# Windowed attention and a gated feed-forward layer: weights converted piece by piece in the order of need, the first steps issued in program order

## The chip, the core and the metric

The kernel runs on one core of one Trainium2 chip. The metric is the device time of the launch in microseconds, as the median of three runs. The profile and its trace come from one profiled execution, whose own time stands in the table below.

## What is computed

```python
def _attn_ref(q, k, v):            # 8 batches, 8 heads, 576 positions, head size 64
    scores = scale * np.matmul(q, k.transpose(0, 1, 3, 2))
    rel = pos[:, None] - pos[None, :]
    mask_plain = (rel >= 0) & (rel < 32)
    mask_dil = (rel >= 0) & (rel < 32 * 4) & (rel % 4 == 0)
    # heads 0 to 3 plain, heads 4 to 7 dilated
    scores = np.where(masks[None], scores, -1e9)
    attn = softmax(scores)
    return np.matmul(attn, v)

def _moe_ref(x, w_in, w_out):      # 4608 tokens, 512 -> 2048 -> 512
    h = x @ w_in
    g = h * np.clip(h + 3.0, 0.0, 6.0) / 6.0
    return g @ w_out
```

The attention's output, with its heads side by side, is the x of the second part. All is float32.

## The kernel before

**The feed-forward part** is cut into 12 chunks c of 384 tokens and 16 blocks f of 128 hidden columns. One step is a pair (c, f). It has a first product gemm1 (lines 407 to 409, twelve matmuls into a PSUM tile ps_h, of which there are two), a stage on ScalarE (ACT) and VectorE (DVE), and a second product gemm2 (lines 428 to 430, nine matmuls into three PSUM tiles ps_o, which add up over all f). Each float32 operand is held as a rounded high part and the remainder, and each product is made of three matmuls: high by high, low by high, high by low. The stage between the products has four instructions: L412 on ACT reads ps_h and writes t, L413 on DVE writes t again, L416 on ACT rounds t into gh, L417 on DVE makes the remainder gl. gemm2 of a step stands two steps behind its gemm1 (LAG).

**The order of the steps.** Chunk 0 leads: the first LEAD steps are (0, 0), (0, 1) and so on, then chunk 0 and chunk 1 take turns, (0, f + LEAD) and (1, f). From step 32 on chunks 2 to 11 follow one another. So a new block f is met first at every second step of this stage, and twice: its first half (from w_in) by gemm1, its second half (from w_out) by gemm2 two steps later.

**The weights.** Each block f has two pieces of 512 KB, its halves. A piece is loaded into a tile st and then converted there into its high and low part in the tile wt of the block: two extractions on ACT (L338, L339) and a shift on DVE (L340), together `cv_fields`; a merge and a custom operation on DVE (L346, L350) and a rounding copy on ACT (L351), together `cv_join`; a subtraction on DVE that makes the low part (L355), `cv_split`. One call of `convert_beat` does one of each for three pieces that follow one another. The pieces are taken in the order of f, both halves of a block together, and gemm1 of a block waits for both (`weights_ready`). All tiles st and wt, and the first nine items' loads, come from one pool of 18 slots.

**The attention** has 48 items (batch, kind of mask, part). An item: scores on TensorE (L163), row maximum, subtraction (L195, L196 on DVE), exponent (L200 on ACT), a transpose of the weights e on TensorE (L242) copied by ACT into a, the product with the values (L173, L181), normalising on DVE (L207, L208, L210), a transpose of the result x, and a split into xh (L299 on ACT) and xl (L302 on POOL), the high and low parts that gemm1 reads. Of the 48 items 12 are done in a start-up of rounds `tau`: round r does the scores of item r, the values of item r - 3, the transposes of e of item r - 1 and of x and the split of item r - 4. Tables by round say where conversion beats (CB) and steps (EARLY) are mixed in. Chunk 0 needs items 0 to 4, chunk 1 items 5 to 9. The other items stand beside later steps, at fixed halves of steps.

**What sets the order on the engines.** The framework's scheduler orders each engine's instructions by a priority number, which `turn_of` sets, and by when it plans their inputs to be ready. All loads are issued by the queue of SyncE (SP), one behind the other.

Names that are used below: round r is `tau`, step n is the n-th pair (c, f), piece k is the k-th half block in the order of conversion, all from 0.

Of the kernel before, what the change touches and what calls it, by code (L numbers as in the profile page):

```python
# [22 lines left out]
TB = 4 * RT  # L23
SPARE = 2
WORK = 12
BEATS = 30
EXTRA = 2
# [12 lines left out]
DEL = 0.2  # L40
G2 = 0.8
EV = -1.9
# [4 lines left out]
def windowed_attention_ffn(ctx: ExitStack, tc: tile.TileContext, qk, vp, w, mask, out):  # L47
# [138 lines left out]
    def softmax(t, ps, masked):  # L186
        e = work_tile("e")
        mx = small.tile([P, SLOTS], F32, name="mx")
        ev = e.rearrange("p (s x) -> p s x", x=2 * QB)
        sv = ps[:, :CH].rearrange("p (s x) -> p s x", x=2 * QB)  # L190
        if not masked:
            _, kind, part = trios[t]
            nc.vector.tensor_tensor(out=e, in0=ps[:, :CH], in1=mask_sb[:, 3 * kind + part], op=ALU.add)
            sv = ev
        nc.vector.tensor_reduce(out=mx, in_=sv, axis=AX.X, op=ALU.max)  # L195
        nc.vector.tensor_tensor(  # L196
            out=ev, in0=sv, in1=mx.rearrange("p (s o) -> p s o", o=1).broadcast_to([P, SLOTS, 2 * QB]),
            op=ALU.subtract,
        )
        nc.scalar.activation(e, e, AF.Exp, scale=SCALE)  # L200
        es[t] = e
        load_qk(t + NLOAD)

    def normalise(t, ps):
        pv = ps[:, : SLOTS * W].rearrange("p (s x) -> p s x", x=W)
# [12 lines left out]
    def blocks():  # L218
        return [(i, u, r) for i in range(SLOTS) for u in range(2) for r in range(2)]

    def st_both(ts, tv):
# [81 lines left out]

    def pace(ins):
# [8 lines left out]

    wt, staged = {}, {}
    WN = w.shape[3]

    def load_w(p):
        st = wpool.tile([P, 4, WN], F32, name="st", tag="w")
# [9 lines left out]
        return words[:, :, 1], words[:, :, 0], st[:, 2], st[:, 3], wt[f][:, 2 * j], wt[f][:, 2 * j + 1]  # L332

    def cv_fields(p):
        if p % 2 == 0:
            wt[p // 2] = wpool.tile([P, 4, WN], F32R, name="wt", tag="w")
        hi_w, lo_w, v, a, _, _ = parts(p)
        pace(nc.scalar.mul(v, hi_w, 2.0**-112))  # L338
        pace(nc.scalar.mul(a.bitcast(U32), lo_w.bitcast(U32), 2.0**-29))  # L339
        nc.vector.tensor_scalar(  # L340
            out=v.bitcast(U32), in0=v.bitcast(U32), scalar1=3, scalar2=None, op0=ALU.logical_shift_left
        )
# [10 lines left out]
    def cv_split(p):  # L353
        _, _, v, _, hi, lo = parts(p)
        nc.vector.tensor_tensor(out=lo, in0=v, in1=hi.bitcast(F32), op=ALU.subtract)  # L355
        del staged[p]


    NP = 2 * NF
    beat = {"loaded": 0, "fields": 0, "join": 0, "split": 0}  # L360

    def load_ahead(n):
        while beat["loaded"] < min(n, NP):
            f = beat["fields"] // 2
            if len(staged) + f + 1 + 1 > NF + SPARE and len(staged) > 0 and beat["loaded"] >= 2:
                break
            load_w(beat["loaded"])
            beat["loaded"] += 1

    def convert_beat():  # L370
        if beat["split"] < beat["join"]:
            cv_split(beat["split"])
            beat["split"] += 1
        if beat["join"] < beat["fields"]:
            cv_join(beat["join"])
            beat["join"] += 1
        p = beat["fields"]
        if p < NP:
            load_ahead(p + 1)
            if p < beat["loaded"]:  # L380
                cv_fields(p)
                beat["fields"] += 1
        load_ahead(p + AHEAD)

    def weights_ready(f):
        while beat["split"] < 2 * (f + 1):
            convert_beat()

    gs, po = {}, {}
# [5 lines left out]
        tc.cur_priority = max(first[0] + int(n * STEP), 0) + 1000  # L395

    def gemm1(n, c, f):
        last["g"] = True
# [5 lines left out]
        for kt in range(NK):  # L404
            a, b = xh[:, kt, r0 : r0 + CH], xl[:, kt, r0 : r0 + CH]
            ks = slice(kt * P, (kt + 1) * P)
            nc.tensor.matmul(ph, lhsT=wt[f][:, 0, ks], rhs=a, start=(kt == 0), stop=False)  # L407
            nc.tensor.matmul(ph, lhsT=wt[f][:, 0, ks], rhs=b, start=False, stop=False)  # L408
            last["pe"] = nc.tensor.matmul(ph, lhsT=wt[f][:, 1, ks], rhs=a, start=False, stop=(kt == NK - 1))  # L409
        turn_of(n + EV)  # L410
        t = work_tile("t")
        nc.scalar.activation(t, ph, AF.Relu, bias=three, scale=1.0)  # L412
# [24 lines left out]
    def first_items(tau):  # L437

        some = lambda t: t if 0 <= t < NFIRST else None
        if some(tau) is not None or some(tau - 3) is not None:  # L440
            st_both(some(tau), some(tau - 3))
        if some(tau - 1) is not None:
            st_turn_e(tau - 1, turn)
        if some(tau - 4) is not None:
            st_turn_x(tau - 4, turn)
            st_split(tau - 4)


    steps = [(0, f) for f in range(LEAD)]
    for f in range(NF):  # L450
        if f + LEAD < NF:
            steps.append((0, f + LEAD))
        steps.append((1, f))
    steps += [(c, f) for c in range(2, NCH) for f in range(NF)]
    beside = {}


# [17 lines left out]
    def step_at(n):  # L475
        c, f = steps[n] if n < len(steps) else (None, None)
        turn_of(n)
        if c is not None:
            gemm1(n, c, f)
        turn_of(n + DEL)  # L480
        for step in beside.get((c, f, 0), []):
            step()
        turn_of(n + 0.4)
        if LEAD <= n < BEATS:
            convert_beat()
        turn_of(n + G2)
        if n >= LAG:
            gemm2(*steps[n - LAG])
# [1 line left out]
        for step in beside.get((c, f, 1), []):  # L490
            step()
        turn_of(n + 0.9)
        if LEAD <= n < BEATS and n % EXTRA == 0:
            convert_beat()

    first[0] = BASE * STEP
    some = P + 2 * CH
# [10 lines left out]
        load_v(t - 2)  # L508
        load_ahead(sum(WITH[: t - 1]))
    n = 0  # L510
    for tau in range(NFIRST + 4):
        turn_of(tau - BASE)
        first_items(tau)
        turn_of(tau - BASE + CD)
        for _ in range(CB.count(tau)):
            convert_beat()
        for _ in range(EARLY.count(tau)):
            step_at(n)
            n += 1
    while n < len(steps) + LAG:  # L520
# [94 lines left out]
```

## Time and profile before

| | us |
|---|---|
| median of 3 runs | 915.86 (915.23 to 916.05) |
| the profiled execution | 915.34 |
| its span, first to last instruction | 913.6 |
| TensorE busy | 891.0 (98%) |
| weight loads of TensorE | 791.6 (87%) |
| VectorE busy | 444.0 (49%) |
| ScalarE busy | 346.5 (38%) |
| POOL busy | 62.5 (7%) |
| mean granted TensorE clock | 0.991 |

Busy times are averages over two stages that differ: a start-up of some 125 us, in which the weights are converted and twelve items done, and a long stage of steps. They are read stage by stage. Matmuls are pipelined, so their busy times overlap; what they cost is read from the starts of neighbours. A wait that the profile ascribes to "issue" is one for which it shows no cause.

### The profile page before, as it was taken

The page shows a single profiled execution, that of the slowest core. Times are in us where ns is not written, and L with a number is a line of the kernel's source. Part 1 is how long each engine was busy: PE and PEld are TensorE (multiplying, and loading weights), DVE is VectorE, ACT ScalarE, POOL GpSimd, SP SyncE. Part 2 cuts the span into 40 slices and gives each one's busy share as a digit, 9 for nine tenths or more (in the row PEclk, how much of TensorE's full clock was granted, in tenths as well). Part 3 has the DMA queues.
Part 4 walks back from the last instruction along what each step waited for, and adds up shares of the span by engine and source line. Part 5 has one row for each costly group of instructions (what it writes and reads, how often), then busy time and mean ns, then how long its engine had stood idle before and what let it go on. Part 6 is the DMA issues. An engine that isn't in the chain of part 4 may idle for free.

```text
span 913.6 us, 20574 instructions
## 1 busy us (share of the span) xinstructions
PE 891.0 (98%) x8732; PEld 791.6 (87%) x8732; DVE 444.0 (49%) x934; ACT 346.5 (38%) x661; POOL 62.5 (7%) x77
## 2 busy tenths in 40 slices
PE   6897999999999999999999999999999999999998
PEld 4576999989889899899888989988888998899996
DVE  3899983244545454444454445445444544422221
ACT  2778862333333333233333223233333332332322
POOL 0212100000010110000000000000100010000000
PEclk9799999999999999999999999999999999999999
DMA  9927430022313222222122123113211310100000
GB/s 354 386 83 260 140 93 0 1 95 89 86 54 119 72 70 81 66 67 84 47 85 85 48 64 104 51 46 99 71 49 52 116 32 11 45 5 1 36 1 34
DMA packets 37820, 74.87 MB, mean 82 GB/s; under 512 B 7264, under 2 KB 16608, under 8 KB 37728
## 3 DMA queue, kind: packets, MB, share of 16 engines
q1 hardware_dynamic: 32544, 64.12, 21.8%
q10 hardware_dynamic: 5184, 9.44, 2.7%
q8 instruction: 68, 1.11, 0.5%
q14 instruction: 24, 0.20, 0.1%
HBM read 57.02 MB, written 9.44 MB: 73 GB/s over the span
## 4 chain that ended last, share of the span: by engine, by line
PE 92%; DMA 4%; DVE 2%; ACT 1%; issue 0%; SPq 0%; POOL 0%
PE ps_o L428 15%; PE ps_h L407 15%; PE ps_h L409 14%; PE ps_h L408 14%; PE ps_o L429 14%; PE ps_o L430 14%; PE ps_a L181 3%; PE ps_a L163 2%; DMA first<-in_v 2%; DMA st<-in_w 1%; DMA v<-in_v 1%; DVE st L350 1%; DVE st L346 1%; DVE wt L355 0%; PE ps_a L242 0%
## 5 line engine op out<-in xcount | busy, mean ns | idle before, releaser
L413 DVE SCALAR_TENSOR_TENSOR t<-t,ps_h 128x384 f32<-128x384 f32 x192 | 106.3, 554 | 326.0 <-ACT t L412 325.8
L407 PE MATMUL ps_h<-xh,wt 128*128 128x384 f32 x768 | 261.5, 341 | 2.9 <-DVE t L413 2.8
L408 PE MATMUL ps_h<-xl,wt 128*128 128x384 f32 x768 | 259.9, 338 | 0.5 <-POOL xl L302 0.5
L409 PE MATMUL ps_h<-xh,wt 128*128 128x384 f32 x768 | 259.9, 338 | 0.0
L428 PE MATMUL ps_o<-wt,gh 128*128 128x512 f32 x576 | 228.7, 397 | 2.0 <-ACT gh L416 2.0
L429 PE MATMUL ps_o<-wt,gh 128*128 128x512 f32 x576 | 224.9, 390 | 0.0
L430 PE MATMUL ps_o<-wt,gl 128*128 128x512 f32 x576 | 221.3, 391 | 0.6 <-DVE gl L417 0.6
L412 ACT ACTIVATE t<-ps_h,three 128x384 f32<-128x384 f32 x192 | 111.1, 579 | 273.3 <-PE ps_h L409 273.0
L417 DVE TENSOR_TENSOR gl<-t,gh 128x384 fp32r<-128x384 f32 x192 | 107.0, 557 | 101.4 <-ACT gh L416 100.1
L407 PEld LDWEIGHTS ps_h<-xh,wt 128*128 128x128 f32 x768 | 144.9, 189 | 11.8 <-DVE t L413 3.3
L408 PEld LDWEIGHTS ps_h<-xl,wt 128*128 128x128 f32 x768 | 144.9, 189 | 8.7 <-POOL xl L302 0.6
L409 PEld LDWEIGHTS ps_h<-xh,wt 128*128 128x128 f32 x768 | 145.0, 189 | 0.8 <-issue 0.3
L416 ACT CAST gh<-t 128x384 fp32r<-128x384 f32 x192 | 98.5, 513 | 111.3 <-DVE t L413 109.1
L430 PEld LDWEIGHTS ps_o<-wt,gl 128*128 128x128 f32 x576 | 108.2, 188 | 24.2 <-DVE gl L417 1.0
L428 PEld LDWEIGHTS ps_o<-wt,gh 128*128 128x128 f32 x576 | 108.3, 188 | 20.1 <-ACT gh L416 2.3
L429 PEld LDWEIGHTS ps_o<-wt,gh 128*128 128x128 f32 x576 | 108.4, 188 | 15.7
L302 POOL TENSOR_TENSOR xl<-xf,xh 128x384 fp32r<-128x384 f32 (+3 forms) x72 | 62.2, 877 | 740.6 <-ACT xh L299 671.8
L200 ACT ACTIVATE e<-e 128x384 f32<-128x384 f32 x48 | 25.2, 526 | 112.4 <-DVE e L196 112.3
L163 PE MATMUL ps_a<-kq 64*32 64x64 f32 x1872 | 47.1, 225 | 0.0
L299 ACT CAST xh<-xf 128x384 fp32r<-128x384 f32 (+3 forms) x72 | 33.7, 536 | 34.7 <-DMA xf<-xf_t 34.6
L181 PEld LDWEIGHTS ps_a<-v,a 64*32 64x32 f32 x1728 | 35.8, 105 | 9.2 <-issue 8.6
L181 PE MATMUL ps_a<-v,a 64*32 64x65 f32 x1728 | 41.6, 225 | 0.0
(45 smaller groups left out, 494.6 us busy)
## 6 DMA issues: line engine op xcount, KB each, us to landing
st<-in_w SPq DMA_DIRECT2D x32, 512.0 KB, 5.7
kq<-in_qk SPq DMA_DIRECT2D x39, 416.0 KB, 4.5
v<-in_v SPq DMA_DIRECT2D x39, 390.0 KB, 3.5
out<-o ACTq DMA_DIRECT2D x36, 256.0 KB, 2.9
first<-in_qk SPq DMA_DIRECT2D x9, 416.0 KB, 8.0
first<-in_v SPq DMA_DIRECT2D x9, 390.0 KB, 8.5
a<-a_t SPq DMA_DIRECT2D x144, 24.0 KB, 1.8
xf<-xf_t SPq DMA_DIRECT2D x144, 24.0 KB, 1.8
```

Of the source, the lines that this page charges most:

```text
L163: last["pe"] = nc.tensor.matmul(ps[at : at + QB, 2 * QB * i : 2 * QB * (i + 1)], lhsT=x[rows, KW + QB * n : KW + QB * (n + 1)], rhs=x[rows ...
L181: last["pe"] = nc.tensor.matmul(ps[at : at + QB, i * W : (i + 1) * W], lhsT=ats[t][rows, QB * n : QB * (n + 1)], rhs=vs[t][rows, n, :], st ...
L407: nc.tensor.matmul(ph, lhsT=wt[f][:, 0, ks], rhs=a, start=(kt == 0), stop=False)
L408: nc.tensor.matmul(ph, lhsT=wt[f][:, 0, ks], rhs=b, start=False, stop=False)
L409: last["pe"] = nc.tensor.matmul(ph, lhsT=wt[f][:, 1, ks], rhs=a, start=False, stop=(kt == NK - 1))
L412: nc.scalar.activation(t, ph, AF.Relu, bias=three, scale=1.0)
L413: nc.vector.scalar_tensor_tensor(out=t, in0=t, scalar=6.0, in1=ph, op0=ALU.min, op1=ALU.mult)
L416: nc.scalar.copy(gh, t)
L417: nc.vector.tensor_tensor(out=gl, in0=t, in1=gh.bitcast(F32), op=ALU.subtract)
L428: nc.tensor.matmul(po[c][tt], lhsT=gh[:, ts], rhs=wt[f][:, 2], start=(f == 0), stop=False)
L429: nc.tensor.matmul(po[c][tt], lhsT=gh[:, ts], rhs=wt[f][:, 3], start=False, stop=False)
L430: last["pe"] = nc.tensor.matmul(po[c][tt], lhsT=gl[:, ts], rhs=wt[f][:, 2], start=False, stop=(f == NF - 1))
```

## The change

- The pieces are taken in the order in which gemm1 and gemm2 first need them (`pieces`): f0 first half, f1 first, f2 first, f0 second, f3 first, f1 second, f2 second, f4 first, f3 second, f5 first and so on. gemm1 waits for the first half of its block alone, gemm2 for the second.
- LEAD is 3 in place of 4. CB has ten beats in rounds 5 to 13 in place of fourteen in rounds 6 to 12, EARLY six steps in place of nine. From step 6 on each step has one beat, between its gemm1 and the reading of its product; the beats that were set by BEATS and EXTRA go.
- Within a beat the order is now: extractions of piece b, merge of piece b - 1, split of piece b - 2, shift of piece b. Where no slot is free for the load of piece b, the split comes first and the load behind it.
- The first loads carry one weight piece per item (WITH), eight in all, where there were up to two and twelve.
- TensorE's instructions stand in program order in the whole kernel, those of DVE and ACT in the rounds and the steps before step 28 (ORDERED).
- In a round the scores' maximum and subtraction come before the normalising, the transposes are placed ahead of the exponent, and the split of x behind the normalising.

```diff
-LEAD = 4
+LEAD = 3
-WITH = (0, 0, 0, 0, 2, 0, 2, 0, 2, 2, 2, 2)
-CB = (6, 6, 7, 7, 8, 8, 9, 9, 10, 10, 11, 11, 12, 12)
+WITH = (0, 0, 0, 0, 1, 1, 1, 1, 1, 1, 1, 1)
+CB = (5, 6, 7, 8, 9, 10, 11, 11, 12, 13)
-EARLY = (8, 9, 10, 11, 12, 13, 14, 15, 15)
+EARLY = (8, 9, 11, 13, 14, 15)
+ORDERED = 28
...
+        if ts is not None:
+            softmax(ts, ps, masked)
+        if between is not None:
+            between()
+        if ts is not None:
+            exponent(ts)
         if tv is not None:
             normalise(tv, pv)
-        if ts is not None:
-            softmax(ts, ps, masked)
...
+    pieces = sorted(range(2 * NF), key=lambda p: (when[p // 2] + LAG * (p % 2), p % 2))
...
     def load_ahead(n):
         while beat["loaded"] < min(n, NP):
-            f = beat["fields"] // 2
-            if len(staged) + f + 1 + 1 > NF + SPARE and len(staged) > 0 and beat["loaded"] >= 2:
+            free = NF + SPARE - len(staged) - len(wt)
+            if len(staged) > 0 and beat["loaded"] >= 2 and free < 1 + (len(wt) < NF):
                 break
-            load_w(beat["loaded"])
+            load_w(pieces[beat["loaded"]])
             beat["loaded"] += 1
...
+        load_ahead(b + 1)
+        full = beat["loaded"] < min(b + 1, NP)
+        if full:
+            cv_split(pieces[b - 2])
+            load_ahead(b + 1)
+        if b < NP:
+            assert b < beat["loaded"]
+            cv_fields(pieces[b])
+        if 0 <= b - 1 < NP:
+            cv_join(pieces[b - 1])
+        if 0 <= b - 2 < NP and not full:
+            cv_split(pieces[b - 2])
+        if b < NP:
+            cv_shift(pieces[b])
+        load_ahead(b + 1 + AHEAD)
...
-        weights_ready(f)
+        weights_ready(2 * f)
...
     def gemm2(c, f):
+        weights_ready(2 * f + 1)
...
         if c is not None:
-            gemm1(n, c, f)
+            ph = gemm1(n, c, f)
+        turn_of(n + 0.4)
+        if n >= len(EARLY):
+            convert_beat()
+        if c is not None:
+            act(n, c, f, ph)
...
-        if LEAD <= n < BEATS and n % EXTRA == 0:
-            convert_beat()
...
+    with tc.manual_schedule(engines={mybir.EngineType.Activation, mybir.EngineType.DVE}):
+        for tau in range(NFIRST + 4):
...
+        while n < ORDERED:
             step_at(n)
             n += 1
...
-        windowed_attention_ffn(tc, *args, o)
+        with tc.manual_schedule(engines={mybir.EngineType.PE}):
+            windowed_attention_ffn(tc, *args, o)
```

The line numbers of the new kernel are shifted: L360, L366, L370 and L375 are the old L340, L346, L350 and L355; L442 and L446 the old L413 and L417.

The order on DVE at the second half of block f3, which gemm2 of step 3 reads. Before, with wt_853 the tile of f3 and t_989 and gl_993 the outputs of step 2:

```order
L417 TENSOR_TENSOR gl_881<-t_877,gh_880 128x384
L346 SCALAR_TENSOR_TENSOR st_151<-st_151 128x512
L355 TENSOR_TENSOR wt_853<-st_145,wt_853 128x512
L350 ISA st_149<-st_149 128x1024
L210 TENSOR_TENSOR x_938<-ps_a_885,z_935 128x384
L196 TENSOR_TENSOR e_940<-ps_a_884,mx_941 128x384
L350 ISA st_151<-st_151 128x1024
L413 SCALAR_TENSOR_TENSOR t_989<-t_989,ps_h_976 128x384
```

And now, with wt_831 the tile of f3, and t_1266 and t_1303 the outputs of steps 4 and 5:

```order
L442 SCALAR_TENSOR_TENSOR t_1266<-t_1266,ps_h_1253 128x384
L446 TENSOR_TENSOR gl_1270<-t_1266,gh_1269 128x384
L442 SCALAR_TENSOR_TENSOR t_1303<-t_1303,ps_h_1290 128x384
L446 TENSOR_TENSOR gl_1307<-t_1303,gh_1306 128x384
L366 SCALAR_TENSOR_TENSOR st_1031<-st_1031 128x512
L370 ISA st_1031<-st_1031 128x1024
L375 TENSOR_TENSOR wt_831<-st_943,wt_831 128x512
```

The subtraction that makes the low part of f3's second half stood ahead of step 2's output, and stands behind step 5's now.

The order on DVE at the second half of block f14. Before, with wt_1711 the tile of f14, and t_1739 and t_1785 the outputs of steps 14 and 15 (f14 is first met by step 24):

```order
L413 SCALAR_TENSOR_TENSOR t_1739<-t_1739,ps_h_1726 128x384
L355 TENSOR_TENSOR wt_1711<-st_1669,wt_1711 128x512
L350 ISA st_1715<-st_1715 128x1024
L417 TENSOR_TENSOR gl_1743<-t_1739,gh_1742 128x384
L413 SCALAR_TENSOR_TENSOR t_1785<-t_1785,ps_h_1772 128x384
L340 TENSOR_SCALAR st_1766<-st_1766 128x512
L346 SCALAR_TENSOR_TENSOR st_1766<-st_1766 128x512
L355 TENSOR_TENSOR wt_1711<-st_1715,wt_1711 128x512
```

And now, with wt_2034 the tile of f15, wt_1956 that of f14, t_2079 and t_2117 the outputs of steps 25 and 26, and st_2032, st_2071 and st_2109 the last three pieces, 29 to 31 (gemm2 of step 25 reads f14 behind gemm1 of step 27):

```order
L442 SCALAR_TENSOR_TENSOR t_2079<-t_2079,ps_h_2057 128x384
L446 TENSOR_TENSOR gl_2083<-t_2079,gh_2082 128x384
L375 TENSOR_TENSOR wt_2034<-st_2032,wt_2034 128x512
L366 SCALAR_TENSOR_TENSOR st_2071<-st_2071 128x512
L370 ISA st_2071<-st_2071 128x1024
L360 TENSOR_SCALAR st_2109<-st_2109 128x512
L442 SCALAR_TENSOR_TENSOR t_2117<-t_2117,ps_h_2095 128x384
L446 TENSOR_TENSOR gl_2121<-t_2117,gh_2120 128x384
L366 SCALAR_TENSOR_TENSOR st_2109<-st_2109 128x512
L370 ISA st_2109<-st_2109 128x1024
L375 TENSOR_TENSOR wt_1956<-st_2071,wt_1956 128x512
```

The last load, of piece 31 into st_2109, takes the slot of st_2032 and waits for its subtraction. On ACT the two extractions of st_2109 stand ahead of the reading of step 26's product, so on DVE everything from the third last of these groups on follows them.

More of the change, by code (lines that the diff above doesn't have):

```diff
@@ L25 @@
 WORK = 12
-BEATS = 30
-EXTRA = 2
 WARM = 8
@@ L302, in st_split @@
             eng.tensor_tensor(out=view(xl), in0=src, in1=view(xh).bitcast(F32), op=ALU.subtract)
+    steps = [(0, f) for f in range(LEAD)]
+    for f in range(NF):
+        if f + LEAD < NF:
+            steps.append((0, f + LEAD))
+        steps.append((1, f))
+    steps += [(c, f) for c in range(2, NCH) for f in range(NF)]
+    when = {f: steps.index((0, f)) for f in range(NF)}
     def pace(ins):
@@ L334, in cv_fields, with cv_shift @@
     def cv_fields(p):
[L335 removed]
+        if p // 2 not in wt:
             wt[p // 2] = wpool.tile([P, 4, WN], F32R, name="wt", tag="w")
         hi_w, lo_w, v, a, _, _ = parts(p)
[L338 to L339 removed]
+        nc.scalar.mul(v, hi_w, 2.0**-112)
+        nc.scalar.mul(a.bitcast(U32), lo_w.bitcast(U32), 2.0**-29)
+    def cv_shift(p):
+        v = parts(p)[2]
         nc.vector.tensor_scalar(
@@ L439, in first_items, with between @@
         some = lambda t: t if 0 <= t < NFIRST else None
[L440 to L443, printed above, removed]
+        def between():
+            if some(tau - 1) is not None:
+                st_turn_e(tau - 1, turn)
+            if some(tau - 4) is not None:
+                st_turn_x(tau - 4, turn)
+        st_both(some(tau), some(tau - 3), between)
         if some(tau - 4) is not None:
-            st_turn_x(tau - 4, turn)
             st_split(tau - 4)
[L449 to L454, printed above, removed]
     beside = {}
```

52 lines of the change are left out of this document (22 added, 30 removed).

## The prediction

> **What bounds the kernel now.** I read the busy time by stage first, then what TensorE (PE) waited for, then the starts of one marker instruction. In the first view the columns are busy time (and instructions) of PE, weight loads, VectorE (DVE), ScalarE (ACT) and POOL, then the granted clock and the DMA share.
>
> ```profile
> 30.00:40.00 10.00, 8.03 (x110) 4.93 (x117) 9.42 (x20) 8.09 (x17) 3.54 (x4) 0.65 1.02 404
> 110.00:120.00 10.00, 10.00 (x52) 9.12 (x51) 10.00 (x20) 7.39 (x14) 0.00 (x0) 1.00 0.34 107
> 200.00:300.00 100.00, 100.00 (x1044) 89.78 (x1044) 51.05 (x114) 34.88 (x68) 8.19 (x10) 1.00 0.29 89
> ```
> ```profile
> PE ps_a L173 <- issue: 9.3, 4, 3.8
> PE ps_h L407 <- DVE t L413: 2.8, 1, 2.8
> ```
>
> From 110 us on PE never pauses; every wait of the whole program lies in the start-up. So the change can win only there, and lose there or wherever it makes PE wait anew. L412 reads each step's finished first product, so its starts tell when product n ended (I call that E(n)). These are steps 6, 16 and 20:
>
> ```profile
> 90.77 0.58 ACT L412 ACTIVATE t<-ps_h,three 128x384 f32<-128x384 f32 x1
> ...
> 131.46 0.58 ACT L412 ACTIVATE t<-ps_h,three 128x384 f32<-128x384 f32 x1 [1.51 <-PE ps_h L409]
> ...
> 147.97 0.58 ACT L412 ACTIVATE t<-ps_h,three 128x384 f32<-128x384 f32 x1 [2.41 <-PE ps_h L409]
> ```
>
> Steps 16 to 20 are (147.97 - 131.46)/4 = 4.13 us apart, PE's own pace. Carried back, a program already at that pace would have E(6) = 147.97 - 14 x 4.13 = 90.15. Both programs do the same PE work behind step 6 (the 12 items are done by then, one transpose apart), so the result is **E(6) of the change against 90.15, plus any new wait behind it**.
>
> **The start-up, step by step.** DVE's groups in the first 125 us (busy, mean ns):
>
> ```profile
> L350 DVE CUSTOM_DVE_ANT_0 st<-st 128x1024 uint16<-128x1024 uint16 x29 | 22.1, 764 | 0.0
> L346 DVE SCALAR_TENSOR_TENSOR st<-st 128x512 uint32<-128x512 uint32 x30 | 22.0, 732 | 0.2
> L355 DVE TENSOR_TENSOR wt<-st,wt 128x512 fp32r<-128x512 f32 x28 | 20.7, 742 | 1.4 <-ACT wt L351 1.4
> L340 DVE TENSOR_SCALAR st<-st 128x512 uint32<-128x512 uint32 x30 | 13.3, 445 | 2.2 <-ACT st L338 2.1
> L413 DVE SCALAR_TENSOR_TENSOR t<-t,ps_h 128x384 f32<-128x384 f32 x14 | 7.6, 546 | 1.7 <-ACT t L412 1.7
> L417 DVE TENSOR_TENSOR gl<-t,gh 128x384 fp32r<-128x384 f32 x14 | 7.6, 545 | 0.0
> L210 DVE TENSOR_TENSOR x<-ps_a,z 128x384 f32<-128x384 f32 x12 | 6.6, 550 | 0.2
> L195 DVE TENSOR_REDUCE mx<-ps_a 128x6 f32<-128x384 f32 x12 | 6.6, 549 | 4.5 <-PE ps_a L163 4.5
> L196 DVE TENSOR_TENSOR e<-ps_a,mx 128x384 f32<-128x384 f32 x12 | 6.6, 549 | 0.1
> L208 DVE RECIPROCAL z<-z 128x6 f32<-128x6 f32 x12 | 2.2, 180 | 0.0
> L207 DVE TENSOR_SCALAR z<-ps_a 128x6 f32<-128x6 f32 x12 | 1.9, 157 | 8.5 <-PE ps_a L173 6.1 <-PE ps_a L163 2.5
> ```
>
> A piece costs DVE 0.764 + 0.732 + 0.742 + 0.445 = 2.68, an item 3 x 0.55 + 0.34 = 1.99 (1.10 of it scores, 0.89 normalising), a step 1.09. What the change removes: in the first 87.3 us, up to the read of product 5, the old order has split 15 pieces (one L355 each, the row below); the new one has split 8 by then, so 7 x 2.68 = 18.8 us of DVE work leave the start-up.
>
> ```profile
> L355 DVE TENSOR_TENSOR wt<-st,wt x15: 644/682/1222, 31.6 to 83.9; 128x512 fp32r<-128x512 f32 x15
> ```
>
> What it adds is waiting, because DVE and ACT now run in program order and L417 stands right behind L413 with ACT's cast between them:
>
> ```profile
> 131.94 0.61 ACT L351 CAST wt<-st 128x512 fp32r<-128x512 f32 x1
> 132.66 0.51 ACT L416 CAST gh<-t 128x384 fp32r<-128x384 f32 x1
> 134.04 0.66 ACT L338 ACTIVATE st<-st 128x512 f32<-128x512 f32 x1 [0.86 <-DMA st<-in_w]
> ```
> ```profile
> 132.08 0.56 DVE L413 SCALAR_TENSOR_TENSOR t<-t,ps_h 128x384 f32<-128x384 f32 x1 [0.74 <-ACT t L412]
> 132.59 0.69 DVE L355 TENSOR_TENSOR wt<-st,wt 128x512 fp32r<-128x512 f32 x1
> 133.21 0.56 DVE L417 TENSOR_TENSOR gl<-t,gh 128x384 fp32r<-128x384 f32 x1
> ```
>
> Step 16 reads: product read 131.46, gl finished 133.77, so **E to gl is 2.31 us** and L413 to the end of L417 is 1.69. The old order puts another piece's split into the hole; the new one leaves it empty.
>
> Where round 7 begins is not changed by this edit, since PE stands still there for a reason that no semaphore shows:
>
> ```profile
> 31.98 0.21 PE L173 MATMUL ps_a<-first,a 64*32 64x65 f32 x1 [3.42 <-issue]
> ```
> ```profile
> 16.00:25.30 9.30, 5.34 (x126) 4.12 (x127) 3.24 (x10) 3.04 (x7) 1.00 (x1) 0.82 1.03 408
> 25.30:29.00 3.70, 2.69 (x127) 2.17 (x127) 2.08 (x5) 3.22 (x6) 1.00 (x1) 1.00 1.02 403
> ```
>
> Between two such waits lie 126 to 127 matmuls with as many weight loads, while the DMA engines are full (1.02): I read it as the instruction stream waiting behind the data. The new order has the same instructions up to there. [...]
>
> So round 7's scores end at about 32.8 and DVE goes on, each round with an item and a piece 1.99 + 2.68 = 4.67, each step 1.69 more: round 7 ends 37.5. Round 8 has step 0, which needs the last of item 4: scores done 38.6; the exponent and two casts to xh, taken as 0.5 each like the cast above, to 40.1; xl on POOL, which starts inside the casts, to 41.6;
>
> ```profile
> 38.35 1.85 POOL L302 TENSOR_TENSOR xl<-xf,xh 128x192 fp32r<-128x192 f32 x2 [4.07 <-ACT xh L299]
> ```
>
> the last five matmuls at the low clock of that stage (0.65) to 43.2; t and gl to 45.5, while DVE had nothing else to do from 42.1. Round 9 ends 51.9, round 10 56.5, round 11 (two pieces, one step) 65.6, round 12 (no scores) 69.2, round 13 74.4, round 14's normalising 75.3; then the last transpose and half a step of PE: **E(5) = 78.0**. Bounds: gap-free DVE work from 32.8 is 5 x 1.99 + 3 x 0.89 + 8 x 2.68 + 5 x 1.09 = 39.5, hence 72.3; further waits of ACT in order could add 4, hence 82.
>
> Then the first new wait. gemm2 of step 3 stands behind product 5 on PE, and needs the split of piece 8, which DVE has behind t and gl of step 5: 2.31 + 0.73 + 0.76 + 0.74 less three overlaps of 0.1, less the first matmul (0.23), which needs the other half: **4.0 us of idle PE**. What such a gap does to the clock is seen once:
>
> ```profile
> 90.00 0.44 PE L407 MATMUL ps_h<-xh,wt 128*128 128x384 f32 x1 [2.82 <-DVE t L413]
> ```
> ```profile
> 91.00:92.00 1.00, 1.00 (x5) 1.00 (x4) 1.00 (x4) 1.00 (x3) 0.00 (x0) 0.53 1.03 422
> 92.00:93.00 1.00, 1.00 (x5) 1.00 (x4) 1.00 (x3) 0.27 (x1) 0.66 (x1) 0.50 1.13 369
> 93.00:94.00 1.00, 1.00 (x6) 0.91 (x5) 1.00 (x3) 0.49 (x2) 0.88 (x1) 0.50 0.79 315
> 94.00:95.00 1.00, 1.00 (x4) 0.80 (x4) 1.00 (x3) 1.00 (x3) 0.00 (x0) 0.76 0.28 115
> ```
> ```profile
> 75.69 0.50 PE L428 MATMUL ps_o<-wt,gh 128*128 128x512 f32 x1 [1.98 <-ACT gh L416]
> ```
>
> 2.82 us of idling were followed by a clock of 0.50 to 0.76, which loses 0.47 + 0.50 + 0.50 + 0.24 = 1.7 us; 1.98 us were not. I take 1.7 for 4 us (bounds 0 and 1.7). So E(6) = 78.0 + 4.13 + 4.0 + 1.7 = 87.8: **2.3 us won**.
>
> **Behind the start-up.** Steps 6 to 26 convert one piece each with ACT in order: L413's wait, gl, join, custom operation, ACT's cast of that piece, and only then the next step's read. That ring is 2.31 + 0.73 + 0.76 + 0.61 = 4.41 without overlap and about 4.1 with 0.1 at each of three seams; against PE's 4.13 it costs between 0 and 0.28 x 20 = 5.6. I take a ring of 4.20, near the overlapped end as neighbouring rows overlap: **1.3 us lost**. The cover is thin: any slip of DVE in a step is PE's.
>
> The last piece is late. Its load takes the place of piece 29 and waits for that split, which stands behind gl of step 25; the landing time of such late loads is
>
> ```profile
> DMA to landing us min/median/max: 3.3/3.7/5.1
> ```
>
> From E(25): gl 2.31, split 0.74, landing 3.7, then ACT in order: two extractions and a cast, 0.57 apart each, 8.5; product 26 is read only then, gl of step 26 at 10.8, join 12.1, split of piece 30 at 12.7. PE wants that split for gemm2 of step 25 at 2 x 4.13 + 0.23 = 8.5: **4.2 us of idling and 1.7 of clock lost** (with 3.3 for the landing 3.8). Before, f14's second half was split some ten steps ahead, so nothing waited. Steps 24 and 25 meet the same wait for pieces 29 and 30, but read their product 0.1 us late only.
>
> Setting PE to program order in the long stage costs nothing by the 200 to 300 us row: items stand at the same halves, gl is done 2.31 after its product and read 8.3 after it.
>
> Sum: -2.3 + 1.3 + 4.2 + 1.7 = +4.9 on the profiled execution's 915.34 (span 913.6 and 1.7 around it): 920.2. The median of the runs, 915.86, is 0.5 higher: **920.5**.
>
> **The rivals.**
> A, faster or equal: the 18.8 us come through. The mechanism is DVE alone in rounds 7 to 14: if ACT and POOL are always ahead and its operations start 0.51 to 0.60 apart as L413 and L355 above do, E(5) comes between 65 and 72.3, and the result is 907 to 915, around 911. It decides from E(5) below 73. For it: DVE is at 9.42 of 10 us in the 30 to 40 us row, so work taken away is time. Against it: the empty holes of each step, and step 0 that cannot be earlier than item 4's xl.
> B, the last load is not late, for the queue finds its slot sooner: 914.6. The order of the split before that load speaks against it.
> C, the fetch wait goes, as the change loads 8 pieces where 12 were loaded at once: round 7 could begin near 30, where DVE's sums for round 6 end, 2.8 earlier, so 917.7. Against: at 32 us neither order has emptied its queue. [...]
> D, PE in program order waits in the long stage, 0.3 us in each of the 36 later items: 931. Nothing in the rows is for it.
> E, gaps of 4 us do not lower the clock, as the 1.98 us one did not: 917.1.
>
> **How the numbers follow.** Forecast 0.50 (its own range 917 to 925), A 0.26, B 0.04, C 0.07, D 0.06, E 0.07. A change below 0.2% (1.8 us) can't be told from none here. Faster: A without its upper end, 0.23; same: that end, B and most of E, 0.13; slower: the rest, 0.64. The range 911 to 926 takes in A's middle, both bounds of E(5) and of the ring, and leaves out D.
>
> **What would show it.** E(5) near 78 and E(6) near 88 by the product reads; two PE waits of about 4 us, the first on the second half of f3, the second near 177 us on f14's; a clock of 0.5 behind each; steps 7 to 23 at 4.13 to 4.25. Wrong it is if E(6) lies before 83, if there is no wait near 177 us, or if PE waits anywhere behind it.

## The result, and the profile after

The change makes the kernel slower. Its median is 930.26 us (930.06 to 932.13, 4 runs) against 915.95 (915.23 to 917.91, 4 runs), a ratio of 1.0157 with a 95% interval of 1.0137 to 1.0178. The direction was forecast, the size was not: 4.9 us more were predicted and 14.3 came, beyond the range (911 to 926). In the profiled executions the span goes from 913.6 to 928.5, by 14.9 us. They are split up below.

What TensorE waited for from 60 us on (us in total, times, longest):

```profile
PE ps_o L459 <- DVE wt L375: 7.8, 2, 4.2
PE ps_a L172 <- ACT a L250: 4.6, 1, 4.6
PE ps_o L458 <- ACT wt L371: 2.1, 1, 2.1
PE ps_a L180 <- DMA a<-a_t: 0.3, 1, 0.3
```

The reads of products 5, 6, 25, 27 and 28 on ACT (start, duration, and in brackets the idle time ahead):

```profile
83.93 0.58 ACT L441 ACTIVATE t<-ps_h,three 128x384 f32<-128x384 f32 x1 [1.08 <-PE ps_h L435]
94.77 0.58 ACT L441 ACTIVATE t<-ps_h,three 128x384 f32<-128x384 f32 x1 [3.99 <-PE ps_h L435]
...
177.42 0.57 ACT L441 ACTIVATE t<-ps_h,three 128x384 f32<-128x384 f32 x1
...
190.02 0.58 ACT L441 ACTIVATE t<-ps_h,three 128x384 f32<-128x384 f32 x1
196.87 0.58 ACT L441 ACTIVATE t<-ps_h,three 128x384 f32<-128x384 f32 x1 [5.01 <-PE ps_h L435]
```

The two places of the waits on PE, on f3's second half and on f14's:

```profile
88.29 0.79 PE L459 MATMUL ps_o<-wt,gh 128*128 128x512 f32 x1 [4.16 <-DVE wt L375]
...
185.98 0.50 PE L458 MATMUL ps_o<-wt,gh 128*128 128x512 f32 x1 [2.13 <-ACT wt L371]
190.12 0.80 PE L459 MATMUL ps_o<-wt,gh 128*128 128x512 f32 x1 [3.64 <-DVE wt L375]
```

The table of stages again, with PE's busy time first and the granted clock behind POOL's:

```profile
180.00:190.00 10.00, 4.35 (x21) 3.43 (x19) 4.99 (x9) 3.22 (x6) 0.00 (x0) 0.94 0.15 52
190.00:200.00 10.00, 9.88 (x37) 8.74 (x38) 2.89 (x6) 2.21 (x5) 0.00 (x0) 0.72 0.00 0
200.00:300.00 100.00, 99.67 (x1086) 89.17 (x1085) 48.01 (x109) 35.65 (x69) 7.18 (x9) 1.00 0.30 91
```

So both waits are at the steps where they were forecast, the second one 7 us and more later in time than the forecast's 177 us, and the long stage is full again. The accounts by the prediction's terms:

| term | predicted | measured | from |
|---|---|---|---|
| product 6 against 90.15 | -2.3 | +4.6 | 94.77 |
| of it: product 5 | at 78.0 | at 83.93 | its read |
| of it: idle, then low clock | 4.0 + 1.7 | 4.16 + 2.55 | 94.77 - 83.93 - 4.13 = 6.71 |
| steps 7 to 27 | +1.3 | +2.4 | 85.0 from product to product start, less 20 x 4.13 |
| wait at step 27: idle, low clock | 4.2 + 1.7 | 6.2 + 2.65 | 12.99 from product 27's end to 28's, less 4.13 |
| long stage and end | 0 | -0.95 | reads 15.9 apart at step 28, spans 14.9 |
| sum | +4.9 | +14.9 | |

The first idle time is that of the view, whose matmul ends are modelled; the second is counted from the starts (the view has 2.13 + 3.64 = 5.77 for it). By the starts the first is 4.33, and 2.4 are left for the low clock behind it.

### The profile page after: what moved, and what is told of

It is laid out like the page before. It is cut to its first block, busy times and chain, and to the rows that moved or that the text cites. A ratio compares the mean times of both kernels' runs of the same rounds, so it can differ in the third digit from the quotient of the medians.

```text
span 928.5 us, 20496 instructions
## 1 busy us (share of the span) xinstructions
PE 892.3 (96%) x8732; PEld 795.1 (86%) x8732; DVE 444.2 (48%) x934; ACT 349.1 (38%) x661; POOL 61.5 (7%) x77
## 4 chain that ended last, share of the span: by engine, by line
PE 87%; DVE 5%; ACT 3%; issue 2%; DMA 1%; SPq 1%; POOL 0%; ACTq 0%; DVEq 0%
PE ps_o L458 14%; PE ps_h L433 14%; PE ps_o L459 13%; PE ps_h L434 13%; PE ps_h L435 13%; PE ps_o L460 13%; PE ps_a L180 3%; PE ps_a L162 2%; DVE st L370 1%; DVE st L366 1%; PE ps_a L247 1%; PE ps_a L172 1%; ACT t L441 1%; DVE t L442 1%; ACT gh L445 1%
## 5 line engine op out<-in xcount | busy, mean ns | idle before, releaser
L442 DVE SCALAR_TENSOR_TENSOR t<-t,ps_h 128x384 f32<-128x384 f32 x192 | 106.4, 554 | 330.1 <-ACT t L441 330.1
L459 PE MATMUL ps_o<-wt,gh 128*128 128x512 f32 x576 | 227.2, 394 | 7.8 <-DVE wt L375 7.8
L458 PE MATMUL ps_o<-wt,gh 128*128 128x512 f32 x576 | 228.9, 397 | 2.1 <-ACT wt L371 2.1
L460 PE MATMUL ps_o<-wt,gl 128*128 128x512 f32 x576 | 226.0, 392 | 0.0
L441 ACT ACTIVATE t<-ps_h,three 128x384 f32<-128x384 f32 x192 | 111.4, 580 | 267.6 <-PE ps_h L435 266.4
L446 DVE TENSOR_TENSOR gl<-t,gh 128x384 fp32r<-128x384 f32 x192 | 107.2, 558 | 115.2 <-ACT gh L445 114.0
L459 PEld LDWEIGHTS ps_o<-wt,gh 128*128 128x128 f32 x576 | 109.0, 189 | 27.4 <-DVE wt L375 11.6
L460 PEld LDWEIGHTS ps_o<-wt,gl 128*128 128x128 f32 x576 | 109.0, 189 | 22.9
L458 PEld LDWEIGHTS ps_o<-wt,gh 128*128 128x128 f32 x576 | 108.7, 189 | 20.8 <-ACT wt L371 2.5
L162 PE MATMUL ps_a<-kq 64*32 64x64 f32 x1872 | 45.9, 225 | 0.0
```

Of the source, the lines that this page charges most:

```text
L162: last["pe"] = nc.tensor.matmul(ps[at : at + QB, 2 * QB * i : 2 * QB * (i + 1)], lhsT=x[rows, KW + QB * n : KW + QB * (n + 1)], rhs=x[rows ...
L442: nc.vector.scalar_tensor_tensor(out=t, in0=t, scalar=6.0, in1=ph, op0=ALU.min, op1=ALU.mult)
L446: nc.vector.tensor_tensor(out=gl, in0=t, in1=gh.bitcast(F32), op=ALU.subtract)
L458: nc.tensor.matmul(po[c][tt], lhsT=gh[:, ts], rhs=wt[f][:, 2], start=(f == 0), stop=False)
L459: nc.tensor.matmul(po[c][tt], lhsT=gh[:, ts], rhs=wt[f][:, 3], start=False, stop=False)
L460: last["pe"] = nc.tensor.matmul(po[c][tt], lhsT=gl[:, ts], rhs=wt[f][:, 2], start=False, stop=(f == NF - 1))
```

## Experiments

Theory L of the runs is the prediction's own idea pushed on: TensorE waits because single splits stand too late on VectorE, and each wait is by itself. Its rivals vary: a shared limit (S), the ring of VectorE and ScalarE (R), the landing of the last load (Q). "Start" means the read of product 1: orders that are the same up to there had it between 51.25 and 53.89 in ten profiles, so a single span says nothing below some 1.3 us either way, and the place is read instead. Runs 1 to 9, 12 and 13 are one execution each; runs 10, 11, 14 and 15 are medians of 6 to 12.

**1. One beat ahead of step 5's outputs.**

```diff
-        if n >= len(EARLY):
+        if n >= len(EARLY) - 1:
```

> One conversion beat moves from behind step 5's outputs to ahead of them; nothing else moves. Theory L (lateness: TensorE waits because the split of a piece stands one beat too late, and each such wait stands by itself): the wait on f3's second half goes, with 4.2 us of idling and 2.5 us of low clock behind it; the read of product 6 moves from 94.77 to about 88.1, the wait near 184 to 190 us on f14 stays as it is, span 928.5 to about 921.8. Rival S (the start-up is VectorE's sum of work, so a beat that is done earlier delays step 5's outputs and the same wait comes back at step 6 or 7): product 6 read later than 92, span 926 to 929.

Measured: span 924.1. The same place on PE:

```profile
85.63 0.50 PE L459 MATMUL ps_o<-wt,gh 128*128 128x512 f32 x1 [0.52 <-DVE wt L375]
```

From product 1 to product 6 it takes 37.14 us in place of 42.49: 5.3 of the 6.7 come back, and the wait on f14 stays. Product 6 is read at 89.86, against 88.1 by L and over 92 by S: L holds and S falls. L's span was 2.3 too low: product 5 comes 1.0 later counted from product 1 (32.65 against 31.65), the start is 0.4 later, and the stage behind step 28 takes 0.8 longer.

**2. One beat in each of rounds 5 to 14.**

```diff
-CB = (5, 6, 7, 8, 9, 10, 11, 11, 12, 13)
+CB = (5, 6, 7, 8, 9, 10, 11, 12, 13, 14)
```

> The second of the two beats of round 11 moves behind step 2's outputs (one beat in each of rounds 5 to 14). The number of beats ahead of step 5 stays. Theory P (in program order ScalarE reads product 2 only behind two beats; TensorE idles 4.6 us for the copy of item 11's weights that stands behind that read, and runs without a pause from there to product 5): product 2 is read at about 64 instead of 66.70, product 5 at about 81.2 instead of 83.93, span about 925.8. Rival S (the sum of VectorE's work up to product 5 sets it): product 5 stays within 0.5 us of 83.93, span 928 to 929.

Measured: span 929.2, with the start 1.6 us later (53.89 against 52.28). From product 1 to product 5: 29.70 in place of 31.65, and of the idle 4.6 us 1.6 are left:

```profile
67.71 0.94 PE L172 MATMUL ps_a<-v,a 64*32 64x65 f32 x48 [1.56 <-ACT a L250]
```

P is right by 2.0 of its 2.7 us, counted from product 1. By its own signs the rival S was met (product 5 at 83.59, and a span over 928): with the start 1.6 us later, neither sign could tell the two apart.

**3. One more beat ahead.** The edit of run 1, and `15` at the end of CB.

> The edit of the first of these runs, and one more beat ahead of step 5, so that every later beat comes one step earlier. Theory L: f3's wait goes (6.7 us), the 0.25 us that gemm2 of every odd step from 7 to 25 waits for a split of its own step goes (2.4 us), and at step 27 the split of piece 30 is due 0.4 us late in place of 6.2 us of idling and 2.65 of low clock (8.4 us won): span about 911.0. Rival R (the ring of ScalarE and VectorE in program order costs its 0.1 to 0.3 us in each step whatever the lead): steps 7 to 27 stay at 4.25, span about 913.4. Rival Q (ScalarE standing behind the landing of the last load holds back the outputs of whatever step it falls into): TensorE waits 4 us or more near step 26 to 28 again, span 916 to 920.

Measured: span 921.1, ten above L and 1.1 above Q's range. The 0.25 us at the odd steps are gone, against R. The beat more ahead is paid for in the start-up: from product 1 to product 6 it takes 39.88 us, 2.7 more than in run 1. And PE now waits for product 25's output (VectorE's L442), which stands behind ScalarE's wait for the last load, as Q had it:

```profile
178.01 0.66 ACT L355 ACTIVATE st<-st 128x512 f32<-128x512 f32 x1 [5.11 <-DMA st<-in_w]
...
179.64 0.58 ACT L441 ACTIVATE t<-ps_h,three 128x384 f32<-128x384 f32 x1
```
```profile
180.86 0.44 PE L433 MATMUL ps_h<-xh,wt 128*128 128x384 f32 x1 [4.06 <-DVE t L442]
```

**4. TensorE in program order to step 27 only.** `EngineType.PE` moves from the block around the whole kernel into the block that ends at step 28.

> TensorE keeps program order through the rounds and steps 0 to 27 and is ordered by the framework from step 28 on. Theory T (the order of TensorE in the long stage costs nothing, and saves 0.85 us at the very end, since the last step's three output tiles end one after the other rather than together): steps 28 to 191 as far apart as in both kernels, span about 929.3. Rival D of the prediction (0.3 us of waiting in each of the 36 later items): span about 918.

Measured: span 923.2, less than the first theory and more than D. Product 27 is read at 189.85 (190.02 in the change), and product 46 is read 9.6 us behind the kernel before, against 15.8 in the change: 6 us won between. At the end of the span it is still 9.6, where the change has won some 0.9 back. I had overlooked that the free order has an effect at step 28 itself. PE takes product 28 in the middle of the wait on f14:

```profile
185.81 0.50 PE L458 MATMUL ps_o<-wt,gh 128*128 128x512 f32 x1 [2.08 <-ACT wt L371]
186.88 0.44 PE L433 MATMUL ps_h<-xh,wt 128*128 128x384 f32 x1 [0.57 <-DVE t L442]
```

D falls by the change's own trace: at step 46 and at step 190 alike its product is read 15.8 us behind the kernel before, so the items between cost nothing.

**5. The next split between the two VectorE instructions of an output, from step 6 on.**

```diff
+        if n >= HOLE and beat["at"] - 2 < NP: cv_split(pieces[beat["at"] - 2])
```

(in `act`, behind L442, with HOLE = 6; the beat leaves that split out.)

> From step 6 on the split of the piece that is next in line stands on VectorE between the two instructions of a step's output (L442, L446), in the 0.65 us that VectorE waits there for ScalarE's rounding; before it stood behind the next piece's merge and custom operation. Nothing else moves, on no engine. Theory V (VectorE's own program order is what is late: its cycle of 1.13 + 0.48 + 0.72 + 0.61 + 0.60 + 0.42 + 0.23 = 4.19 us, and 4.8 where the split stands ahead of a load, is longer than TensorE's 4.13, so that the splits come late at every odd step and the last load by over 2 us): the cycle falls to some 3.6, the odd steps' 0.25 goes (2.4 us), the wait of 6.2 us and the low clock of 2.65 behind it near f14 go; up to product 6 nothing changes; span about 917.2, give or take 1 for the start. Rival R (ScalarE's chain sets the cycle): steps at 4.25 as before and a wait of 3 us or more on f14, span 922 or more.

Measured: span 921.6, start 0.6 later. The odd steps' loss is gone. In the waits view it had never stood, since the modelled end of a pipelined matmul covers a gap of 0.1 us; the starts of neighbours show it. The change first (L458 to L459 0.36 us, L459 to L460 0.34), then this run (0.23 and 0.23):

```profile
98.69 0.40 PE L458 MATMUL ps_o<-wt,gh 128*128 128x512 f32 x1
99.05 0.50 PE L459 MATMUL ps_o<-wt,gh 128*128 128x512 f32 x1
99.39 0.39 PE L460 MATMUL ps_o<-wt,gl 128*128 128x512 f32 x1
```
```profile
100.20 0.39 PE L458 MATMUL ps_o<-wt,gh 128*128 128x512 f32 x1
100.43 0.39 PE L459 MATMUL ps_o<-wt,gh 128*128 128x512 f32 x1
100.66 0.39 PE L460 MATMUL ps_o<-wt,gl 128*128 128x512 f32 x1
```

V is right on that. On f14 2.2 us are left, and the products are still read 4.21 us apart, each a little later behind its end (0.1 us at product 7, 1.6 at product 25): R is right on the cycle, which runs through ScalarE, and on the span.

**6. VectorE and ScalarE in the framework's order from step 6 on.** `ORDERED = 6`.

> VectorE and ScalarE keep program order to step 5 only; from step 6 the framework orders them, TensorE as in the change. Theory V (what costs behind step 6 is the fixed order on VectorE, with its empty hole): the waits at odd steps and on f14 go as in the run before this one, span 916 to 919. Rival L2 (the conversion is one beat short whatever the order within a step): the wait on f14 stays at 4 us or more, span 924 or more.

Measured: span 918.2; products 8 to 28 read 4.13 apart, and no wait for a split behind f3's. V holds, L2 falls.

**7. TensorE in the framework's order throughout.**

> The framework orders TensorE in the whole kernel; ScalarE and VectorE as in the change. Theory H (each late split costs as much as it does since TensorE, in program order, cannot take the next product while it waits): from 5 us at f14 alone, which the run with program order to step 28 has shown, to 11 of the 15.6 us of both waits come back, span 918 to 924. Rival T2 (the splits are late by themselves, and another order only moves the wait): f3's wait stays above 3 us and the span above 926, or the framework's order of the rounds costs more than it gives.

Measured: span 920.1, within H's range. From product 1 to product 6: 38.17 in place of 42.49; single waits are smaller (3.2 us the longest behind 60 us, on f14; at most 1.6 elsewhere). H holds, T2 falls.

**8. POOL's part of the start-up on VectorE.** `ONV = tuple(range(12))`.

> The low part of x of the first twelve items is made on VectorE instead of POOL. Theory C (VectorE's two-input operations take 0.5 to 0.9 us longer while POOL works on its subtraction; 6.2 us in all between 30 and 77 us in the changed kernel, where the prediction had 1.8): with POOL empty all custom operations of the rounds take 0.69 and all splits and merges 0.68, and the 12 items add some 7 us of VectorE's own work, so that product 5 is read within 2 us of 83.93. Rival M (the long ones come from the full DMA or from waits inside the operation): durations of 1.2 to 1.4 stay, and product 5 is read 4 us or more later.

Measured: span 929.8, product 5 at 84.06. The custom operation between 27 and 78 us (shortest/median/longest ns), in the change and in this run:

```profile
L370 DVE CUSTOM_DVE_ANT_0 st<-st x9: 692/1209/1379, 30.9 to 74.8; 128x1024 uint16<-128x1024 uint16 x9
```
```profile
L370 DVE CUSTOM_DVE_ANT_0 st<-st x9: 691/692/693, 31.8 to 74.6; 128x1024 uint16<-128x1024 uint16 x9
```

C holds, M falls. Over all conversion operations between 27 and 78 us the excess in the change is 6.7 us.

**9 and 10. Runs 1 and 6 together, and then with run 2.**

> Two edits that were run apart, together: one beat ahead of step 5's outputs (5.9 us between product 4 and product 6), and the framework's order on VectorE and ScalarE from step 6 on (span 918.2, with f3's wait still in it). If the waits are separate, as theories L and V have it, span 918.2 - 5.9 = 912.3, give or take 1.2 for the start of round 7 and 8, which has varied by that much between runs of the same order. If they share their cause (a beat more ahead moves the same wait elsewhere): 916 or more.

> The same with one beat in each of rounds 5 to 14, as in the second run, which read product 5 2.0 us earlier counted from product 1: span 910.3, time 912.0, ratio to the kernel before 0.996. If what was won in the second run is only paid back behind product 5: 912 to 914 and a ratio of 0.998 to 1.000.

Measured: span 916.7 for the first; time 917.58 for the second, ratio 1.0017 (1.0008 to 1.0025). Both miss what theory L gave (912.3, and 912.0 with 0.996): they did not add up. With the order free from step 6 on, VectorE's sequence has pieces of later beats ahead of the outputs of steps 3 to 5, and f3's wait is back:

```profile
88.17 0.50 PE L459 MATMUL ps_o<-wt,gh 128*128 128x512 f32 x1 [2.01 <-DVE wt L375]
```

Whether that is a shared limit was open until runs 12 to 15.

**11. The kernel before, TensorE in program order in the last step alone.**

> The kernel before, with TensorE in program order in the very last step alone. Theory T (the part of the change that set TensorE to program order wins 0.85 us at the very end, since the three output tiles of the last step end one after the other): 0.8 us less than before, ratio 0.9991. Rival: the end is set by the last output transfer in both orders: ratio 1.000.

Measured: 915.5 against 916.26, ratio 0.9987 (0.9978 to 0.9997): T, by a small margin. ACT idles 3.95 us ahead of the last output copies in the kernel before, and 3.05 here.

**12. Runs 1 and 5 together (HOLE = 5), in program order.**

> Two edits that were run apart, together, in program order throughout: one beat ahead of step 5's outputs, and the next piece's split between the two VectorE instructions of each output from step 5 on. Theory L + V (the waits are lateness on VectorE, each by itself; the earlier pair did not add up since the framework then moved later beats ahead of step 4's and 5's outputs): no more than 1 us left of f3's wait, none at the odd steps, some 2 us near f14; span 928.5 - 5.9 - 2.4 - 6.7 = 913.5, give or take 1.2 for the start. Rival S (a shared limit: work taken from one place returns at another): 916 or more.

Measured: span 915.9, 0.8 of it from the start. Place by place it is as L and V say: 0.8 us left on f3, none at the odd steps, 2.6 on f14. The span is 2.4 higher than expected and at the edge of the rival's 916: the start is 0.8 later, and product 5 comes 1.5 later counted from product 1 (33.11 against 31.65). Run 12 alone does not decide between L and S.

**13. The next product's read ahead of the rounding copy on ScalarE.**

```diff
-            convert_beat()
+            convert_beat(n < HOLE)
...
+        if n >= HOLE and beat["at"] - 2 < NP: cv_last(pieces[beat["at"] - 2])
```

(`cv_join` leaves the copy out where its argument is false; `cv_last` does the copy, which now stands behind L441, and the split.)

> The same, and ScalarE reads the next product (L441) ahead of the rounding copy of the piece in hand, in place of behind it; no other engine's order changes. Theory A (what is left near f14, 2 us, is ScalarE's ring of 4.2 us: its rounding copy waits 0.8 us in every step for the custom operation, and the product's read behind it): products from step 6 on are read 4.13 us apart and within 0.1 us of their end, no wait near f14, span about 911.3. Rival Q (the landing of the last load holds it): 1.5 us or more stay near f14, span 913 or more.

Measured: span 912.8. Products 6 to 25 are read 4.13 apart, and 0.3 us are left on f14, though ScalarE waits for the last load as before:

```profile
168.29 0.58 ACT L441 ACTIVATE t<-ps_h,three 128x384 f32<-128x384 f32 x1 [1.26 <-PE ps_h L435]
...
173.77 0.66 ACT L355 ACTIVATE st<-st 128x512 f32<-128x512 f32 x1 [3.76 <-DMA st<-in_w]
```

A holds, Q falls: with the reads ahead of it on time, this landing (3.76 us of waiting on ScalarE) left TensorE 0.3 us.

**14. The same with run 2's beats.**

> The same with one beat in each of rounds 5 to 14: product 5 read 2 us earlier counted from product 1, as in the second run. Theories L, V and A: span about 909.3, time 911, ratio to the kernel before 0.995. If the 2 us are paid back behind product 5, as when the framework set the order: ratio 0.997 to 0.999.

Measured: 914.34 against 915.98, ratio 0.9983 (0.9973 to 0.9994), the second of the two outcomes. Product 5 is read 31.15 us after product 1, 1.2 earlier than in run 13, and that was more than paid back at f3 (2.15 us idle and some 1.7 of low clock):

```profile
85.19 0.50 PE L459 MATMUL ps_o<-wt,gh 128*128 128x512 f32 x1 [2.15 <-DVE wt L375]
```

**15. The split of piece 8 in step 4's output** (HOLE = 4, and `cv_last` copies only what is not copied yet).

> One instruction moves against the third of the last runs: the split of piece 8 (f3's second half) stands in step 4's output instead of behind the next piece's merge and custom operation. Theory L (spreading the beats moved product 5 two us ahead of that split, so that f3's wait came back with 2.3 us of idling and 1.7 of low clock): that wait goes, product 6 is read at about 87.0, span 913.5 - 4.0 = 909.5, time 911.3, ratio to the kernel before 0.995. Rival S (the 2 us come back at another place once more): 912.5 or more, ratio 0.998 or more.

Measured: 909.6 against 915.69, ratio 0.993 (0.9915 to 0.9944), span 908.0: faster than both kernels, and some 20 us below the change. From 60 us on, PE waited for this only:

```profile
PE ps_a L172 <- ACT a L250: 1.6, 1, 1.6
PE ps_a L247 <- ACT xh L304: 0.3, 1, 0.3
```
```profile
80.00:90.00 10.00, 10.00 (x54) 9.25 (x53) 9.68 (x17) 8.19 (x17) 1.06 (x1) 1.00 0.69 269
```

One instruction of VectorE, moved past three others, is worth some 4.7 us here. L holds and S falls.

## Why the prediction was wrong

**The mechanism of the two waits was right.** f3's and f14's second half, both on the named splits, both followed by a clock of 0.5; the long stage without waits; D false. The forecast of slower came from them, and not from the start-up, which was to win 2.3 us and lost 4.6. Of the 10.0 us between the forecast 4.9 and the measured 14.9, 5.9 are product 5's read, 1.0 f3's wait, 1.1 the steps, 2.9 f14's wait, and 0.9 came back at the end.

**The step that failed is the walk through the start-up**, "E(5) = 78.0", with its upper bound of 82. Product 5 was read at 83.93. Three things were missing.

First, VectorE's conversion operations were priced at their means over 125 us. In the rounds each item's subtraction on POOL lies on top of one or two of them and makes them up to 0.75 us longer. One such round:

```profile
49.87 1.31 POOL L307 TENSOR_TENSOR xl<-xf,xh 128x384 fp32r<-128x384 f32 x1 [5.77 <-ACT xh L304]
```
```profile
49.63 0.68 DVE L366 SCALAR_TENSOR_TENSOR st<-st 128x512 uint32<-128x512 uint32 x1
50.35 1.38 DVE L370 CUSTOM_DVE_ANT_0 st<-st 128x1024 uint16<-128x1024 uint16 x1
51.65 0.68 DVE L375 TENSOR_TENSOR wt<-st,wt 128x512 fp32r<-128x512 f32 x1
```

The walk had some 1.8 us for this, the trace has 6.7 between 27 and 78 us, and run 8 shows the cause. With round 7's scores 1.0 later than taken (33.84 against 32.8) that explains how the walk fell behind: 1.8 us at the end of round 7, 2.7 at round 9, 3.5 at round 11, 4.6 at round 14. In the round above the custom operation took 1.38 us beside the subtraction; the one at 65.45 us, with none beside it, took 0.69.

Second, ScalarE's place in the order. Product 2's last matmul starts at 60.19, its read only at 66.70, behind the ScalarE work of two beats. The copy of item 11's weights stands behind that read, and TensorE stands for it:

```profile
66.70 0.57 ACT L441 ACTIVATE t<-ps_h,three 128x384 f32<-128x384 f32 x1
67.90 0.51 ACT L445 CAST gh<-t 128x384 fp32r<-128x384 f32 x1 [0.62 <-DVE t L442]
68.32 0.47 ACT L250 COPY a<-ps_a 128x384 f32<-128x384 f32 x1
```
```profile
68.84 0.96 PE L172 MATMUL ps_a<-v,a 64*32 64x65 f32 x38 [4.59 <-ACT a L250]
```

Third, from there PE works 15.1 us without a pause to product 5, and it does so at a granted clock of 0.5 from 69.31 to 72.72 us, behind the idling of 4.59, which by an estimate from that clock costs 1.7 of the 15.1; the walk had no low clock there. The walk followed VectorE alone and gave the end 2.7 us behind round 14; it took 4.0. Run 2 shows this part by itself: the same VectorE work, 2.0 us less. Run 8 has every conversion operation at its short duration, the subtractions added, and product 5 where it was (84.06). How much earlier product 5 would come with neither on VectorE, no run shows, so the shares of the three in the 5.9 us stay open.

**New wait 1** was right in place and idling (4.16 against 4.0), with the low clock 2.55 in place of 1.7, which had been its upper bound. 1.7 us is an estimate of what one stretch of 3.41 us at 0.5 costs, half its length; here there were two on end, of which 1.91 us fell into the idling (see the last section). Run 6 has the same idling of 4.16 us at this place with one stretch, and from product 5's end to product 6's it loses 6.0 us in place of 6.7. So the length of the gap did not tell whether one stretch or two would come.

**The ring** (1.3 us) was right in length (4.20 forecast, products read 4.21 apart in run 5) and wrong in where it acts. In the change products 6 to 22 are read 4.26 apart, as TensorE's own steps are. The prediction looked at the product's read; what PE stood for was the split, which gemm2 of each odd step reads in the very step that makes it. Run 5 removed that without touching the cycle. And the cycle's other effect was left out: where the split is put ahead of a load the cycle is 4.8 us, and the reads of products 23, 24 and 25 slip to 0.8, 1.4 and 2.1 us behind their ends. "But read their product 0.1 us late only" is the second step that failed:

```profile
174.94 0.34 PE L435 MATMUL ps_h<-xh,wt 128*128 128x384 f32 x1
```

is product 25's last matmul, and its read stands above at 177.42, 2.1 us behind the end of that matmul (174.94 + 0.34). That delay goes straight into the last load, so **new wait 2** is 6.2 us of idling in place of 4.2, and its low clock 2.65. Runs 5, 12 and 13 take it away in two parts, 6.6 us by the split and 2.3 by the read's place.

**PE's program order** was taken as free. Beside the items it is; at the end it wins some 0.8 us (run 11, interval 0.3 to 2.0); behind step 27 it costs 6 us by barring PE from the next product (run 4). The prediction had counted that as part of the wait without seeing that the order causes it.

**Rivals**: A and B did not come; C neither, the waits for "issue" are 10.4 us against 9.3 (that they are the instruction stream waiting behind the data was the author's reading, which no run tested); E is refuted by both low clocks.

**Slips in the sums**, all small: 20 steps at 4.20 less 4.13 are 1.4 and not 1.3; 920.2 and 0.5 are 920.7 and not 920.5; L355 and L417 in A's rows start 0.62 apart and not 0.60.

Of the points of the change, the runs undid the program order alone: TensorE's (4, 7) and, from step 6 on, that of VectorE and ScalarE (6). What each of the others costs or wins by itself is not shown.

## What to carry to other kernels

Where engines run in program order, write for each step the time at which each operand is made and the time at which it is read, and leave a spare of more than one operation: a split that is due in the step that makes it turns any slip into idling. A hole that one engine leaves while it waits for another is where the next step's operand belongs. Judge an edit of this size by the interval between two fixed events as well as by the span, since a start that varies by 2.6 us from end to end hides 2.

## What the runs showed of the hardware

**Low clock.** Between 54 and 206 us the kernel before has one stretch at a granted clock of 0.5, from 91.07 to 94.48, 3.41 us long. The change has four, which begin at 55.66, 69.31, 86.38 and 188.78: the first two lasted 3.41 us, the last two 6.83, and from one beginning to the next it is 4, 5 and 30 times 3.413 us (the last 102.40). The one behind f3's wait in run 14, from 86.33 to 89.74, lasted 3.41 too. (Read from rows of 0.25 us, in run 14 of 0.5 us. Below are rows of 0.5 us of the change with the beginnings and ends of its last three: busy time of PE, granted clock, DMA share, GB/s.)

```profile
69.00:69.50 0.50, 0.50 (x38) 0.81 0.00 0
72.50:73.00 0.50, 0.50 (x4) 0.78 0.72 254
86.00:86.50 0.50, 0.00 (x0) 0.88 0.18 74
93.00:93.50 0.50, 0.50 (x4) 0.80 0.00 0
188.50:189.00 0.50, 0.00 (x0) 0.78 0.00 0
195.50:196.00 0.50, 0.50 (x4) 0.90 0.00 0
```

The length of a gap did not tell by itself what followed it. In the change the 4.59 us ahead of 68.84 were followed by 3.41 us at 0.5, and the 4.16 us ahead of f3's split by 6.83, of which 1.91 (86.38 to 88.29) fell into the idling; in run 6 the 4.16 us there were followed by 3.41 (90.61 to 94.02). What decides it is not shown. In the change's third stretch gemm1's matmuls start 0.32 us apart, and 0.17 behind it; so the estimate for a stretch of 3.41 us that TensorE works through is 1.7 us, half of it, and nothing more for the part that falls into the idling.

**POOL was no free engine here.** The subtractions on POOL cost VectorE 6.7 us between 27 and 78 us. Done by VectorE itself (run 8) they cost about as much: its busy time from 27 to 84 us is 47.3 us there and 45.9 in the change, and the kernel's time is the same within the start's spread.
